# Attention and feed-forward in one kernel: w_out loaded in two column parts, the weight fold moved behind the scores of batch 0, batches 1 and 2 moved among the outputs of group 0

## The chip, the cores and the metric

The kernel runs on one core of a Trainium2 chip. The metric is the device time of one execution in microseconds (us). A core has five engines with their own instruction queues, each worked off in order: TensorE (PE: matmuls, with weight loads beside them, PEld), VectorE (DVE), ScalarE (ACT), GpSimd (POOL) and SyncE (SP). DMA transfers are issued from the queues of POOL, SP and ACT; those that change the type on the way (all loads here, float32 to float16) are issued from POOL. Engines wait for one another by semaphores. Matmul results go to PSUM, eight banks of 512 float32 per partition.

## The reference

Sliding-window causal attention over 8 batches, 8 heads, 576 positions and head size 64 gives the rows of x; a feed-forward part follows. Cut to what matters:

```python
scores = (q @ k.T) / sqrt(64)
mask = (rel >= 0) & (rel < 64)              # rel = query position - key position
attn = softmax(where(mask, scores, -1e9))
x = (attn @ v) -> [4608 tokens, 512]        # heads side by side
a = x @ w1                                  # [512, 1024]
b = x @ w2                                  # [512, 1024]
h = a * b @ w3                              # [1024, 1024]
out = h @ w_out                             # [1024, 512]
```

## The kernel before

**The fold.** w3 and w_out are multiplied once into wc (1024 x 512), so that each token needs x @ w1, x @ w2, the product of both, and one product with wc. w3 comes in four parts of 256 rows (`load_w3`, L447), w_out in one load (`load_wo`, L441). `fold_t(fc)` transposes 128 rows of w3 in 8 matmuls against the identity (L454) and DVE copies them out (L456); `fold_mm(fc)` multiplies them with w_out in 8 matmuls (L462) and DVE or ACT copies the result into `wc_sb` (L463). There are 8 values of fc.

**Attention.** Each batch has three segments of 192 queries; segment n of all is number n (0 to 23). `load_qk` loads q or k of a batch in four transfers (L206), each row of which holds RUN = 9 positions; DVE transposes it in two halves (`transposes`, L217). `scores(n)` makes 32 small matmuls (L276) into two PSUM tiles named a_ps, of which there are only two, of two banks each. `weigh` takes the exponential of each on ACT (L286), the first for index d = 2n and the second for 2n+1. The mask is applied by two or four selections on POOL (`select`, L250 and L252); for the odd d of batches 0 and 1 (SHORT = 2) DVE multiplies with a band of ones instead (L291), made once on POOL by `make_bands`. `values(d)` multiplies with v and, in the same matmuls, with ones beside v, whose result is the sum of the weights. It uses an a_ps tile again; ACT takes the logarithm of the sum and the exponential of its negative, and DVE multiplies into xT. In batches below SHORT this has a short form with 16 matmuls, two ACT steps and one DVE step (L320 to L328); in the others 8 matmuls, three ACT steps and two DVE steps (L336 to L346). `load_v` loads v in blocks (L230), `copy_v` copies half blocks on DVE (L234, L236). `ones_of` writes the ones beside v. `keep_sums` stores the logarithms for a range check at the end.

**Feed-forward.** Nine groups g of 512 tokens. `ffn_ab(g, fc)` has 8 matmuls of 512 columns (L398) into two of the four f_ps tiles; ACT copies one out (L403) and DVE multiplies the other into `ab` (L404). For group 1 it is done in pieces of two fc and 256 tokens, first for the first token half and later for the second. `ffn_o(g, t)` makes 128 rows of the output in 8 matmuls (L416), copied out by DVE (L418) and stored from SP (L425).

**The order.** Nothing schedules by itself: each engine runs its part of the code in the order in which the code is written. `keep_busy` runs matmuls on the identity at the start. Then come the loads, the scores of batch 0 between the steps of the fold, values of batch 0, `ffn_ab(0)`, and the outputs of group 0 with batch 1 among them. From there on the order is a loop over slots (one ffn_ab or ffn_o each, with a due time), after each of which ticks u run while they are due. There are 12 ticks to a batch: tick 4n calls `scores(n)` with both exponentials, the two ticks after it `values` of the segment before, and the table `late` says in which tick of a batch the loads, transposes and copies of the next batches are issued. All loads of the program share eight semaphores in turn, so a load is issued only when the eighth load before it has landed, and what stands behind it in POOL's queue waits with it.

Of the kernel before, what the change touches and what calls it, by code (L numbers as in the profile page):

```python
# [9 lines left out]
FP16 = mybir.dt.float16  # L10
# [5 lines left out]
P = 128  # L16
# [128 lines left out]
def kernel(  # L145
# [52 lines left out]

    RUN = 9

    def load_qk(b, which):
        src = k if which == "k" else q
        r = RUN
        t = sb.tile([P, 2, TI * D], FP16, name=which + "16", bufs=2)
        for j in range(NJ):
            nc.gpsimd.dma_start(  # L206
                out=t[32 * j:32 * j + 32].rearrange("p hh (i n) -> p (hh i) n", n=r * D),
                in_=src[b, 2 * j:2 * j + 2].rearrange("hh (i p r) d -> p (hh i) (r d)", p=32, r=r))
        t16s[which, b] = t
# [51 lines left out]

    def scores(n):
# [20 lines left out]
    def weigh(d, s_ps, si, w):  # L283

# [63 lines left out]
    def keep_sums(n):  # L348
# [4 lines left out]

    late = {1: [("t", 1, "k", 0)], 3: [("t", 1, "q", 0), ("v", 1, 0, 2, 3)],
            5: [("t", 1, "k", 1), ("v", 1, 4, 5)], 6: [("load", 2, "k")], 7: [("t", 1, "q", 1)],
            8: [("copy", 1, 4)], 9: [("copy", 1, 1)], 10: [("load", 2, "q")]}

# [8 lines left out]
    def tick(u):  # L366
# [82 lines left out]
    def fold_t(fc):  # L449
# [40 lines left out]
    nc.scalar.preload_act_table_set("natural_log_exp_and_others")  # L490
    make_identity(nc, ident16)
# [6 lines left out]
    def fold_step(fc):  # L498
        if fc + 1 < 8:
            w3Ts[fc + 1] = fold_t(fc + 1)  # L500
        fold_mm(fc, w3Ts.pop(fc), act_cp if fc % 4 == 3 else dve_cp)
# [8 lines left out]
    ones_of(0, nc.vector)  # L510
    make_bands()
    ones_of(1, nc.gpsimd)
    keep_busy(100)
    for hh in range(2):
        transposes(0, "k", hh)
        transposes(0, "q", hh)
# [3 lines left out]
    load_w3(3)  # L520
    w3Ts[0] = fold_t(0)
    fold_step(0)
    scores(1)
# [10 lines left out]
    copy_v(0, 1)
    fold_step(4)
    copy_v(0, 4)
    values(0)
    values(1)
    fold_step(5)
    values(2)  # L540
    values(3)
    fold_step(6)
    values(4)
    values(5)
    fold_step(7)
# [11 lines left out]
    transposes(1, "q", 0)
    transposes(1, "q", 1)
    scores(3)
    load_qk(2, "q")  # L560
# [6 lines left out]
    load_v(2, 0, 2, 3, 4, 5)
    ffn_o(0, 2)
    store()
    scores(5)  # L570
    values(8)
    values(9)
# [4 lines left out]
    for fc in range(0, 8, 2):
        ffn_ab(1, fc, 2, 0, 256)
        transposes(2, "kq"[fc // 4], fc // 2 % 2)
        if fc in (2, 4):  # L580
            values(9 + fc // 2)
# [71 lines left out]
```

## Time and profile before

| | us |
|---|---|
| median of 3 runs | 295.2 |
| lowest, highest | 294.61, 295.31 |
| the profiled execution | 294.81 |
| its span in the trace | 293.1 |
| PE busy | 262.6 |
| DVE, POOL, ACT busy | 182.8, 175.8, 149.6 |

The profile is of one execution. Its times are microseconds from the start of the span. A line such as L398 is a line of the kernel before. The mean granted clock of TensorE is 0.961 of full speed; the two levels are 1.2 and 2.4 GHz, so that a mean between 0.5 and 1 is a mix of both.

### The profile page before, as it was taken

How to read it: one execution, taken by the hardware profiler on the slowest of the kernel's cores; microseconds unless marked ns; L12 is line 12 of the kernel's file. 1: busy time of each engine (PE TensorE's matmuls, PEld its weight loads, DVE VectorE, ACT ScalarE, POOL GpSimd, SP SyncE). 2: the span in 40 equal slices, each digit the busy share in tenths (PEclk: the TensorE clock that was granted, in tenths of full speed). 3: DMA queues.
4: the chain of work that ended last, by engine and by line, in shares of the span. 5: the costliest groups of instructions: out<-in, count | busy, mean ns of one | idle time of the engine just before them, and what ended most of it. 6: DMA issues, size and time to landing. Idle time of an engine off the chain costs nothing.

```text
span 293.1 us, 6430 instructions
## 1 busy us (share of the span) xinstructions
PE 262.6 (90%) x2518; PEld 151.2 (52%) x2518; DVE 182.8 (62%) x272; ACT 149.6 (51%) x256; POOL 175.8 (60%) x243
## 2 busy tenths in 40 slices
PE   7729999962899579999999999999999999999992
PEld 7624564421478445545554498554545554454442
DVE  3424674556479557778688847766988655645531
ACT  1023264322745825786677576567658875551310
POOL 8894927209762997878779872957765554104000
PEclk9968999996899959999999999999999999999998
DMA  6999999916983778859885668395843012003013
GB/s 80 182 211 155 183 192 173 114 38 118 117 141 64 46 66 148 151 35 146 173 74 48 121 170 55 28 226 85 54 85 90 4 38 108 1 2 144 1 39 113
DMA packets 56419, 29.45 MB, mean 100 GB/s; under 512 B 39312, under 2 KB 50832, under 8 KB 56384
## 3 DMA queue, kind: packets, MB, share of 16 engines
q0 software_dynamic: 50960, 19.41, 60.7%
q1 hardware_dynamic: 5280, 9.46, 8.9%
q8 instruction: 21, 0.34, 0.5%
q14 instruction: 14, 0.11, 0.1%
q10 hardware_dynamic: 144, 0.13, 0.1%
HBM read 38.80 MB, written 9.44 MB: 165 GB/s over the span
## 4 chain that ended last, share of the span: by engine, by line
PE 79%; DVE 6%; DMA 4%; ACT 4%; issue 2%; POOL 2%; DVEq 0%; POOLq 0%
PE f_ps L398 40%; PE f_ps L416 21%; PE a_ps L276 5%; PE f_ps L462 5%; PE a_ps L336 4%; DMA ab<-in_moe_w_dram 4%; ACT pt L286 2%; PE a_ps L320 2%; DVE kT L217 1%; PE f_ps L454 1%; DVE xT L346 1%; POOL k L206 1%; DVE qT L217 1%; POOL q L206 1%; DVE ab L404 1%
## 5 line engine op out<-in xcount | busy, mean ns | idle before, releaser
L398 PE MATMUL f_ps<-xT,w_sb 128*128 128x512 f16 (+1 forms) x704 | 132.3, 340 | 0.8 <-DVE ab L404 0.8
L398 PEld LDWEIGHTS <-w_sb 128*128 128x128 f16 x704 | 66.6, 98 | 52.3 <-issue 2.7
L250 POOL TENSOR_SCALAR_AFFINE_SELECT pt<-pt 128x1024 f16<-128x1024 f16 (+2 forms) x56 | 45.9, 819 | 61.6 <-ACT pt L286 61.6
L286 ACT ACTIVATE pt<-a_ps 128x1024 f16<-128x1024 f32 (+1 forms) x48 | 43.1, 950 | 64.4 <-PE a_ps L276 64.4
L404 DVE TENSOR_TENSOR ab<-f_ps,a_sb 128x512 f16<-128x512 f32 x72 | 49.4, 690 | 36.2 <-PE f_ps L398 20.4
L416 PE MATMUL f_ps<-wc_sb,ab 128*128 128x512 f16 (+1 forms) x296 | 69.3, 384 | 0.1
L403 ACT COPY a_sb<-f_ps 128x512 f32<-128x512 f32 x72 | 41.9, 582 | 36.6 <-PE f_ps L398 36.6
L252 POOL TENSOR_SCALAR_AFFINE_SELECT pt<-pt 128x1024 f16<-128x1024 f16 (+2 forms) x56 | 46.6, 833 | 3.8
L416 PEld LDWEIGHTS <-ab 128*128 128x128 f16 x296 | 28.2, 100 | 31.8 <-issue 3.0
L230 POOL DMA_DIRECT2D v<-in_v_dram x40 | 34.0, 859 | 0.6 <-PE f_ps L416 0.2
L345 DVE TENSOR_TENSOR xT<-a_ps,r 64x384 f16<-64x384 f32 x36 | 19.7, 546 | 23.5 <-ACT r L344 23.5
L418 DVE COPY t2k<-f_ps 128x512 f32<-128x512 f32 (+1 forms) x36 | 24.2, 681 | 12.7 <-PE f_ps L416 12.1
L276 PE MATMUL a_ps<-qT,kT 32*128 32x128 f16 (+1 forms) x768 | 17.2, 214 | 9.7 <-DVE qT L217 5.6
L342 ACT ACTIVATE ln_s<-a_ps 64x384 f32<-64x384 f32 x36 | 17.6, 488 | 13.2 <-PE a_ps L336 12.2
L336 PEld LDWEIGHTS <-v 128*128 128x128 f16 x288 | 18.5, 99 | 8.6 <-issue 2.0
L217 DVE STREAM_TRANSPOSE kT<-k 128x576 int32<-128x576 int32 x16 | 19.5, 1221 | 5.4 <-DMA k<-in_k_dram 5.1
L276 PEld LDWEIGHTS <-kT 32*128 32x128 f16 x768 | 12.6, 94 | 19.5 <-issue 17.6
L336 PE MATMUL a_ps<-pt,v 128*128 128x128 f16 (+1 forms) x288 | 21.1, 217 | 1.3 <-POOL pt L252 1.3
L206 POOL DMA_DIRECT2D q<-in_q_dram x32 | 17.7, 559 | 7.0 <-DMA w_sb<-in_moe_w_dram 6.9
L346 DVE TENSOR_TENSOR xT<-a_ps,r 64x384 f16<-64x384 f32 x36 | 20.2, 560 | 0.5
L217 DVE STREAM_TRANSPOSE qT<-q 128x576 int32<-128x576 int32 x16 | 19.2, 1208 | 1.8 <-DMA q<-in_q_dram 1.7
L206 POOL DMA_DIRECT2D k<-in_k_dram x32 | 17.8, 564 | 2.8 <-issue 1.7
(46 smaller groups left out, 171.4 us busy)
## 6 DMA issues: line engine op xcount, KB each, us to landing
out_dram<-t2k SPq DMA_DIRECT2D x35, 256.0 KB
k<-in_k_dram POOLq DMA_DIRECT2D x32, 144.0 KB, 4.9
q<-in_q_dram POOLq DMA_DIRECT2D x32, 144.0 KB, 4.6
v<-in_v_dram POOLq DMA_DIRECT2D x32, 128.0 KB, 4.6
w_sb<-in_moe_w_dram POOLq DMA_DIRECT2D x4, 512.0 KB, 7.8
ab<-in_moe_w_out_dram POOLq DMA_DIRECT2D x1, 1024.0 KB, 11.5
ab<-in_moe_w_dram POOLq DMA_DIRECT2D x2, 512.0 KB, 13.8
xT<-in_moe_w_dram POOLq DMA_DIRECT2D x2, 512.0 KB, 13.2
```

Of the source, the lines that this page charges most:

```text
L206: nc.gpsimd.dma_start(out=t[32 * j:32 * j + 32].rearrange("p hh (i n) -> p (hh i) n", n=r * D), in_=src[b, 2 * j:2 * j + 2].rearrange("hh ...
L217: nc.vector.transpose(dst[b][:, hh].rearrange("q t c -> q (t c)").bitcast(I32).rearrange("q (i p r) -> q i r p", p=32, r=r), t16s[which, b ...
L230: nc.gpsimd.dma_start(out=vh[lo:P, c], in_=v[b, :, s0:s0 + P - lo, :].rearrange("h s d -> s h d"))
L250: nc.gpsimd.affine_select(out=sl, in_=sl, pattern=pat, compare_op=ALU.is_ge, fill=0.0, base=off, channel_multiplier=-1)
L252: nc.gpsimd.affine_select(out=sl, in_=sl, pattern=[[-s, m] for s, m in pat], compare_op=ALU.is_ge, fill=0.0, base=63 - off, channel_multip ...
L276: nc.tensor.matmul(s_ps[j // 2][:, j % 2, o0:o0 + m], kT[part, a, k0:k0 + P, c], qT[part, a, q0:q0 + m, c], start=(c == 0), stop=(c == 1), ...
L286: nc.scalar.activation(pt[:, :, :, 0:w], s_ps, AF.Exp, bias=-SHIFT, scale=scale)
L336: nc.tensor.matmul(o_ps[:, jj, o0:o0 + n], v16[:, si * 2 + bi, j0 + jj, a * D:a * D + P], pt[:, jj, a, c0:c0 + n], start=first, stop=(bi = ...
L398: nc.tensor.matmul(d[:, f * n + c0:f * n + c1], w[:, dc, (fc + f) * P:(fc + f + 1) * P], xT[:, dc, xc:xc + c1 - c0], start=first, stop=(dc ...
L403: act_cp(a_sb[:, 0:nf * n], a_ps[:, 0:nf * n])
L404: nc.vector.tensor_tensor(ab[:, fc:fc + nf, lo:hi], b_ps[:, 0:nf * n].rearrange("p (f n) -> p f n", f=nf), a_sb[:, 0:nf * n].rearrange("p ...
L416: nc.tensor.matmul(o_ps[:, 0:c1 - c0], ab[:, fc, t * P:t * P + P], wc_sb[:, fc, c0:c1], start=(fc == 0), stop=(fc == 7))
```

## The change

w_out is loaded in two halves of its columns, and the first four products of the fold are done by halves. The bands are made between the loads of w3's first and second part, the identity after the loads of k, and the ones of both v tiles on DVE. scores(1) and scores(2) come between the transposes and the products of the fold; the results of the fold are copied by ACT alone. All transposes of batch 1 lie inside ffn_ab(0); scores(3), (4) and (5) stand between the outputs of group 0 and its values behind them, together with the transposes of batch 2; k and q of batch 2 are loaded before that in one row. The first scores of batch 2 move between the first pieces of group 1. Batch 2 takes the short form of values (SHORT = 3), but the band product on DVE stays with batches 0 and 1 (EARLY = 2). In the loop the second exponential of a segment is issued a tick later (tick 4n+1), and the table `late` puts the transposes into ticks 3, 4, 7 and 8. Batches 3 to 7 load q and k with rows of RUN = 2 positions. The third output of group 0 is copied by ACT.

```diff
-    SHORT = 2
+    SHORT = 3
+    EARLY = 2
-    RUN = 9
+    RUN = [9] * 3 + [2] * (B - 3)
...
+        r = RUN[b]
...
         for jp in range(2):
-            weigh(2 * n + jp, s_ps[jp].rearrange("k j (a n) -> k j a n", a=2)[:, :, :, 0:w], si, w)
+            held[2 * n + jp] = s_ps[jp].rearrange("k j (a n) -> k j a n", a=2)[:, :, :, 0:w]
+        weigh(2 * n)
+        if now:
+            weigh(2 * n + 1)
...
-        if d % 2 == 1 and d < 6 * SHORT:
+        if d % 2 == 1 and d < 6 * EARLY:
...
-    late = {1: [("t", 1, "k", 0)], 3: [("t", 1, "q", 0), ("v", 1, 0, 2, 3)],
+    late = {3: [("t", 1, "k", 0), ("v", 1, 0, 2, 3)], 4: [("t", 1, "q", 0)],
...
         if m == 0 and n < NS:
-            scores(n)
+            scores(n, now=False)
+        if m == 1 and n < NS:
+            weigh(2 * n + 1)
...
-    def ffn_o(g, t):
+    def ffn_o(g, t, cp=dve_cp):
...
-    def load_wo():
-        nc.gpsimd.dma_start(out=wo16, in_=moe_w_out.rearrange("(e p) m -> p e m", p=P))
+    def load_wo(half):
+        cols = slice(half * 256, half * 256 + 256)
+        nc.gpsimd.dma_start(out=wo16[:, :, cols], in_=moe_w_out[:, cols].rearrange("(e p) m -> p e m", p=P))
...
-    def fold_mm(fc, w3T, cp):
+    def fold_mm(fc, c0, c1, cp):
         o_ps = ps_f.tile([P, DM], FP32, name="f_ps")
         for ec in range(8):
-            nc.tensor.matmul(o_ps, w3T[:, ec, :], wo16[:, ec, :], start=(ec == 0), stop=(ec == 7))
-        cp(wc_sb[:, fc, :], o_ps)
+            nc.tensor.matmul(o_ps[:, c0:c1], w3Ts[fc][:, ec, :], wo16[:, ec, c0:c1], start=(ec == 0), stop=(ec == 7))
+        cp(wc_sb[:, fc, c0:c1], o_ps[:, c0:c1])
...
+    keep_busy(120)
     scores(0)
+    keep_busy(30)
+    fold_t(0)
+    fold_t(1)
+    scores(1)
...
+    fold_mm(0, 0, 256, act_cp)
+    fold_mm(1, 0, 256, act_cp)
+    fold_t(2)
+    fold_t(3)
+    scores(2)
...
-            ahead = (LAG + 1) * (min(1, (i + 1) / 4) if g == 1 else 1)
-            slots.append((w, lo + (hi - lo) * (i + 1) / len(part) + ahead))
-    u = 24
+            due = lo + (hi - lo) * (i + 1) / len(part) + LAG + 1
+            slots.append((w, [28, 29, 30, 32, 33, 34, 36, 37][i] if g == 1 else due))
+    u = U0
```

Where the order changes, the rows of the engines' queues show it. First POOL at the start of the program, from the load of w_out on (tile ab is w_out or w3, as the right side says; band is the mask of ones). Before:

```order
L441 DMA ab_83<-in_moe_w_out_dram 128x8x512
L447 DMA ab_84<-in_moe_w3_dram 128x2x1024 x2
L447 DMA xT_77<-in_moe_w3_dram 128x2x1024
L230 DMA v16_0_79<-in_v_dram 128x8x64 x3
L259 MEMSET band_0_81 128x256
```

And now:

```order
L461 DMA ab_83<-in_moe_w_out_dram 128x8x256
L467 DMA ab_84<-in_moe_w3_dram 128x2x1024
L267 MEMSET band_0_81 128x256
L258 AFFINE_SELECT band_0_81<-band_0_81 128x128
L260 AFFINE_SELECT band_0_81<-band_0_81 128x128
L258 AFFINE_SELECT band_0_81<-band_0_81 128x64
L260 AFFINE_SELECT band_0_81<-band_0_81 128x64
L267 MEMSET band_1_82 128x256
L258 AFFINE_SELECT band_1_82<-band_1_82 128x256
L260 AFFINE_SELECT band_1_82<-band_1_82 128x256
L467 DMA ab_84<-in_moe_w3_dram 128x2x1024
L461 DMA ab_83<-in_moe_w_out_dram 128x8x256
```

Half of w_out moved behind the second part of w3, and the bands from behind the loads to between them.

Next DVE around the outputs of group 0 (t2k is an output on its way out, kT and qT the transposed k and q, pt the weights, ab the product of the feed-forward). Before, from the last pieces of ffn_ab(0) on:

```order
L217 STREAM_TRANSPOSE kT_801<-k16_494 128x2x9x32
L404 TENSOR_TENSOR ab_722<-f_ps_818,a_sb_827 128x512
L418 COPY t2k_830<-f_ps_831 128x512
L217 STREAM_TRANSPOSE qT_842<-q16_499 128x2x9x32 x2
L291 TENSOR_TENSOR pt_885<-pt_885,band_0_81 128x4x192
L418 COPY t2k_893<-f_ps_894 128x512
L291 TENSOR_TENSOR pt_943<-pt_943,band_1_82 128x1024
L234 COPY v16_1_80<-v16_1_80 64x8x64
L236 COPY v16_1_80<-v16_1_80 64x8x64
L328 TENSOR_TENSOR xT_77<-a_ps_948,r_950 128x2x192
```

And now, from the copies of v on:

```order
L242 COPY v16_1_80<-v16_1_80 64x8x64
L308 TENSOR_TENSOR pt_932<-pt_932,band_0_81 128x4x192
L437 COPY t2k_935<-f_ps_936 128x512
L308 TENSOR_TENSOR pt_985<-pt_985,band_1_82 128x1024
L437 COPY t2k_991<-f_ps_992 128x512
L308 TENSOR_TENSOR pt_1041<-pt_1041,band_1_82 128x1024
L225 STREAM_TRANSPOSE kT_1044<-k16_879 128x2x9x32
L345 TENSOR_TENSOR xT_77<-a_ps_1058,r_1060 128x2x192
L225 STREAM_TRANSPOSE kT_1044<-k16_879 128x2x9x32
L345 TENSOR_TENSOR xT_77<-a_ps_1081,r_1082 128x2x192
L437 COPY t2k_1104<-f_ps_1105 128x512
```

The transposes of batch 1 (q16_499 before) left this place, the copies of v moved ahead of the bands, and the transposes of batch 2 (k16_879) stand between the products into xT.

Last ACT at the same place (a_ps is the input of an exponential into pt, or of the logarithm of values). Before:

```order
L286 ACTIVATE pt_939<-a_ps_905 128x1024
L286 ACTIVATE pt_943<-a_ps_906 128x1024
L326 ACTIVATE ln_s_949<-a_ps_948 128x384
L327 ACTIVATE r_950<-ln_s_949 128x384
L326 ACTIVATE ln_s_949<-a_ps_970 128x384
L327 ACTIVATE r_971<-ln_s_949 128x384
L286 ACTIVATE pt_1042<-a_ps_1008 128x1024
L286 ACTIVATE pt_1046<-a_ps_1009 128x1024
```

And now:

```order
L303 ACTIVATE pt_981<-a_ps_947 128x1024
L303 ACTIVATE pt_985<-a_ps_948 128x1024
L303 ACTIVATE pt_1037<-a_ps_1003 128x1024
L303 ACTIVATE pt_1041<-a_ps_1004 128x1024
L437 COPY t2k_1046<-f_ps_1047 128x512
L343 ACTIVATE ln_s_1059<-a_ps_1058 128x384
L344 ACTIVATE r_1060<-ln_s_1059 128x384
L343 ACTIVATE ln_s_1059<-a_ps_1081 128x384
```

All exponentials of batch 1 moved ahead of the first logarithm of its values.

## Rows read from the trace of the kernel before

**Rows 1.** Busy time by stages: stretch, its length, engines busy, PEclk granted, DMA share, GB/s

```profile
12.20:20.30 8.10, 0.75 (x33) 0.56 (x32) 3.81 (x4) 1.51 (x2) 7.61 (x14) 0.83 1.19 209
20.30:45.10 24.80, 24.26 (x288) 14.01 (x289) 14.32 (x25) 10.21 (x17) 14.12 (x19) 0.92 1.53 180
24.00:28.00 4.00, 4.00 (x61) 1.98 (x62) 0.95 (x2) 1.94 (x2) 1.13 (x2) 0.96 3.08 139
45.10:61.00 15.90, 15.82 (x73) 7.04 (x72) 8.15 (x12) 5.27 (x9) 6.96 (x10) 1.00 1.26 119
61.00:92.30 31.30, 21.71 (x328) 15.10 (x327) 20.66 (x28) 13.94 (x23) 17.82 (x25) 0.89 0.82 111
92.30:115.40 23.10, 18.02 (x189) 11.50 (x178) 14.63 (x23) 12.90 (x21) 21.40 (x29) 0.85 0.64 68
115.40:288.00 172.60, 171.39 (x1483) 92.44 (x1482) 117.05 (x182) 104.49 (x183) 97.56 (x128) 1.00 0.50 84
```

**Rows 2.** What PE waited for: us in total, times, longest us

```profile
PE a_ps L276 <- DVE qT L217: 5.6, 4, 1.9
...
PE a_ps L320 <- DVE v L236: 4.3, 1, 4.3
PE a_ps L276 <- DVE xT L346: 4.0, 3, 2.8
```

**Rows 3.** Chain of waits up to ffn_ab(0): start us, us, what

```profile
7.14 13.12 DMA ab<-in_moe_w_dram
...
20.30 1.89 PE f_ps L454 x16
22.19 2.90 PE f_ps L462 x8
...
25.67 0.55 PE f_ps L454 x8
26.22 1.73 PE f_ps L462 x8
...
39.12 1.01 PE a_ps L320 x32
...
43.43 1.83 PE f_ps L462 x8
45.26 13.93 PE f_ps L398 x64
```

**Rows 4.** DMA issues of the page: count, KB each, median us to landing

```profile
ab<-in_moe_w_out_dram POOLq DMA_DIRECT2D x1, 1024.0 KB, 11.5
```

**Rows 5.** Timeline and chain: start us, us, engine, operation, idle before and releaser

```profile
9.34 1.22 DVE L217 STREAM_TRANSPOSE kT<-k 128x576 int32<-128x576 int32 x1 [5.11 <-DMA k<-in_k_dram]
...
42.56 0.55 POOL L206 DMA_DIRECT2D q<-in_q_dram  x1 [3.80 <-DMA w_sb<-in_moe_w_dram]
...
66.76 1.95 ACT pt L286 x2
```

**Rows 6.** Chain of waits among the outputs of groups 0 and 1

```profile
66.09 0.62 PE a_ps L276 x32
...
81.65 3.49 PE f_ps L398 x32
...
87.57 0.57 PE a_ps L320 x16
...
105.48 3.53 PE f_ps L416 x8
...
111.56 0.45 PE a_ps L336 x8
```

**Rows 7.** Busy time in one batch of the steady part, columns as in rows 1

```profile
115.39:141.93 26.54, 26.11 (x242) 13.26 (x243) 20.67 (x33) 18.38 (x32) 21.38 (x30) 1.00 0.79 110
```

**Rows 8.** Issues of q and v on POOL: duration ns min/median/max, first and last start

```profile
L206 POOL DMA_DIRECT2D q<-in_q_dram x32: 545/545/642, 4.1 to 200.1; - x32
L230 POOL DMA_DIRECT2D v<-in_v_dram x40: 704/892/910, 10.2 to 216.5; - x40
```

More of the change, by code (lines that the diff above doesn't have):

```diff
@@ L197, with load_qk @@
     t16s, kTs, qTs = {}, {}, {}
-    RUN = 9
-    def load_qk(b, which):
+    RUN = [9] * 3 + [2] * (B - 3)
+    def load_qk(b, which, *hhs):
         src = k if which == "k" else q
[L203 to L209, printed above, removed]
+        r = RUN[b]
+        if (which, b) not in t16s:
+            t16s[which, b] = sb.tile([P, 2, TI * D], FP16, name=which + "16", bufs=2)
+        t = t16s[which, b]
+        if not hhs:
+            for j in range(NJ):
+                nc.gpsimd.dma_start(
+                    out=t[32 * j:32 * j + 32].rearrange("p hh (i n) -> p (hh i) n", n=r * D),
+                    in_=src[b, 2 * j:2 * j + 2].rearrange("hh (i p r) d -> p (hh i) (r d)", p=32, r=r))
+        for hh in hhs:
+            for i in range(2):
+                nc.gpsimd.dma_start(
+                    out=t[:, hh, i * r * D:(i + 1) * r * D],
+                    in_=src[b, hh:H:2, i * 32 * r:(i + 1) * 32 * r].rearrange("j (p r) d -> j p (r d)", p=32, r=r))
     def transposes(b, which, hh):
         dst = kTs if which == "k" else qTs
-        r = RUN
+        r = RUN[b]
         if hh == 0:
@@ L260, in make_bands, with scores @@
             select(bands[i].unsqueeze(1), i)
-    def scores(n):
+    held = {}
+    def scores(n, now=True):
         b, si = divmod(n, 3)
@@ L351, in keep_sums @@
         nc.sync.dma_start(out=lnsum[2 * n:2 * n + 2, :], in_=y[0:P:D].rearrange("a j n -> a (j n)"))
[L354 to L356 removed]
+    late = {3: [("t", 1, "k", 0), ("v", 1, 0, 2, 3)], 4: [("t", 1, "q", 0)],
+            5: [("v", 1, 4, 5)], 7: [("t", 1, "k", 1), ("load", 2, "k")], 8: [("t", 1, "q", 1), ("copy", 1, 4)],
+            9: [("load", 2, "q")], 11: [("copy", 1, 1)]}
     def event(b, kind, ahead, *a):
@@ L410, in ffn_o @@
         r0 = g * GT + t * P
-        halves = [(0, DM, dve_cp)] if (g, t) != (NG - 1, 3) else [(0, 256, act_cp), (256, DM, dve_cp)]
+        halves = [(0, DM, cp)] if (g, t) != (NG - 1, 3) else [(0, 256, act_cp), (256, DM, dve_cp)]
         for c0, c1, cp in halves:
@@ L490 @@
     nc.scalar.preload_act_table_set("natural_log_exp_and_others")
-    make_identity(nc, ident16)
     def ones_of(i, engine):
@@ L496 @@
     w3Ts = {}
[L498 to L501, printed above, removed]
     load_qk(0, "k")
+    make_identity(nc, ident16)
     load_qk(0, "q")
-    load_wo()
+    load_wo(0)
     load_w3(0)
+    make_bands()
     load_w3(1)
+    load_wo(1)
     load_w3(2)
     load_v(0, 0, 2, 3)
[L510 to L516, printed above, removed]
@@ L517 @@
-    keep_busy(40)
-    scores(0)
-    load_v(0, 4, 5)
[L520 to L523, printed above, removed]
+    for i in range(2):
+        ones_of(i, nc.vector)
+    for which in "kq":
+        for hh in range(2):
+            transposes(0, which, hh)
+    keep_busy(120)
+    scores(0)
+    keep_busy(30)
+    fold_t(0)
+    fold_t(1)
+    scores(1)
+    load_w3(3)
+    load_v(0, 4, 5)
+    fold_mm(0, 0, 256, act_cp)
+    fold_mm(1, 0, 256, act_cp)
+    fold_t(2)
+    fold_t(3)
@@ L524 @@
+    scores(2)
     for i in range(2):
         load_w12(i, 0)
-    fold_step(1)
-    scores(2)
+    fold_mm(2, 0, 256, act_cp)
+    fold_mm(3, 0, 256, act_cp)
+    fold_mm(0, 256, DM, act_cp)
+    fold_mm(1, 256, DM, act_cp)
+    fold_t(4)
+    fold_t(5)
+    fold_mm(2, 256, DM, act_cp)
+    fold_mm(3, 256, DM, act_cp)
+    copy_v(0, 1)
+    fold_mm(4, 0, DM, act_cp)
+    values(0)
+    values(1)
+    fold_t(6)
+    fold_mm(5, 0, DM, act_cp)
+    values(2)
+    values(3)
+    copy_v(0, 4)
+    fold_t(7)
@@ L528 @@
+    fold_mm(6, 0, DM, act_cp)
+    values(4)
+    values(5)
+    fold_mm(7, 0, DM, act_cp)
     for i in range(2):
         load_w12(i, 1)
-    fold_step(2)
-    fold_step(3)
     load_qk(1, "k")
     load_qk(1, "q")
[L534 to L545, printed above, removed]
     load_v(1, 0, 2, 3, 4, 5)
-    load_qk(2, "k")
     for n in range(3):
         keep_sums(n)
-    for fc in range(6):
+    for fc in range(8):
@@ L551 @@
         ffn_ab(0, fc)
-    for fc in range(6, 8):
-        transposes(1, "k", fc - 6)
-        ffn_ab(0, fc)
+        if 2 <= fc < 6:
+            transposes(1, "kkqq"[fc - 2], fc % 2)
+    load_qk(2, "k")
+    load_qk(2, "q")
+    copy_v(1, 1)
+    copy_v(1, 4)
+    scores(3)
     ffn_o(0, 0)
     store()
[L557 to L560, printed above, removed]
+    scores(4)
+    load_v(2, 0, 2, 3)
     ffn_o(0, 1)
     store()
-    scores(4)
-    copy_v(1, 1)
+    scores(5)
@@ L565 @@
+    transposes(2, "k", 0)
+    ffn_o(0, 2, act_cp)
+    store()
     values(6)
+    transposes(2, "k", 1)
     values(7)
[L567 to L572, printed above, removed]
+    load_v(2, 4, 5)
     ffn_o(0, 3)
     store()
-    copy_v(1, 4)
+    values(8)
+    transposes(2, "q", 0)
+    values(9)
     load_qk(3, "k")
[L577 to L581, printed above, removed]
+    load_qk(3, "q")
@@ L582 @@
+    ffn_ab(1, 0, 2, 0, 256)
+    values(10)
+    transposes(2, "q", 1)
+    ffn_ab(1, 2, 2, 0, 256)
+    values(11)
+    for n in range(3, 6):
+        keep_sums(n)
+    U0 = 24
+    ffn_ab(1, 4, 2, 0, 256)
+    tick(24)
+    tick(25)
     copy_v(2, 1)
     copy_v(2, 4)
-    load_qk(3, "q")
-    for n in range(3, 6):
-        keep_sums(n)
+    ffn_ab(1, 6, 2, 0, 256)
+    tick(26)
+    U0 = 27
     need = [12 * B if g == NG - 1 else 12 * g + 4 * -(-(GT - 64 * g) // 192) for g in range(NG)]
```

10 lines of the change are left out of this document (6 added, 4 removed).

## The prediction

> **What bounds the kernel now.** I read the span cut into stages first, then what TensorE (PE) waited for, then the chain of waits. From 115.4 us on, PE is busy 171.4 of 172.6 us at a granted clock of 1.00 [rows 1]: whatever the other engines do there, at most 1.2 us can be had. Before that there are three weak stretches: 12.2 to 20.3 (PE busy 0.75 of 8.1 us), 61.0 to 92.3 (21.7 of 31.3, clock 0.89) and 92.3 to 115.4 (18.0 of 23.1, clock 0.85). Between the first two PE is busy nearly all the time [rows 1]. So the kernel is bound by PE's own work, plus some 25 us of the first 115 in which PE waits or runs slowly, and there the change has to be priced. Behind the waits stand other engines: transposes of q on VectorE (DVE), copies of v on DVE, and the DVE products that free the a_ps buffers (5.6, 4.3 and 4.0 us) [rows 2].
>
> The profiled execution took 294.8 us (span 293.1 and 1.7 around it), the median of the runs is 295.2. What I work out in the trace is taken off the median.
>
> **Part 1, the start and the fold.** In the chain, the load of w3's first part is issued at 7.14 and lands 13.12 later, at 20.3; then the first transposes of the fold start [rows 3]. All of w_out (1024 KB) stands ahead of it in the queue [rows 4]; in the new order only one column half does. In 12.2 to 20.3 the queue moved 209 GB/s [rows 1], so 512 KB are 2.5 us and the transposes can start at 17.8. The other bound: shorter rows may move more slowly, and the slowest stretch, the one with the v loads, moved 139 GB/s [rows 1]; then the half takes 3.8 us and the start is at 19.1. I take 209, since a half row of w_out is still four times a row of v. The bands now stand between w3's first and second part on GpSimd; the queue holds data until 17.8, so that costs nothing.
>
> From there to the first matmul of ffn_ab(0) the old order took from 20.3 to 45.3 [rows 3]. The work in it at full clock: 8 transpose groups at 0.55 (4.4), 8 products at 1.73 to 1.83, on average 1.78 (14.2), 2 scores at 0.62 (1.2), 3 pairs of values at 1.01 (3.0): 22.8 us [rows 3, 6]. The rest of the 25.0 is mostly the clock: 16 transposes took 1.89 and the first product 2.90, where 1.10 and 1.73 would do [rows 3], that is 2.0. The new order has four products in two halves, four more pieces at 0.1 each (1.83 against 1.73 after a change of kind): 23.2. It puts scores(1) and scores(2) between transposes and products, which gives loads and copies time, and it copies out on ScalarE (ACT), where nothing is late. So ffn_ab(0) starts at 17.8 + 23.2 = 41.0 instead of 45.3: **-4.3 us**. The identity behind the k loads and the second memset on DVE cost nothing: DVE waits 5.11 us for k there [rows 5] and the memset is as long as the one already in front of it. Without that wait the memset would delay the transposes by its own length.
>
> **Part 2, group 0's outputs, up to the first piece of group 1's second token half.** ffn_ab(0) takes 13.9 us [rows 3] and ends at 54.9 instead of 59.2. All four transposes of batch 1 now lie inside it; what they need is q of batch 1. In the old kernel its third load was issued only at 42.56, after a wait of 3.80 for the weights [rows 5]. By the bytes between w3's first part and it (5.4 MB at 209 GB/s and 0.6 MB of v at 139) it is in at 48, with pauses as in the old queue at 51; DVE reaches it at 51. That is tight, but PE has two products ahead there. Then, up to the point at which the old kernel stood at 92.3, PE has: scores 4 x 0.62 = 2.5; outputs 4 x 1.83 = 7.3; values 6 x 0.57 = 3.4; half pieces of ffn_ab(1) 5 x 1.85 (3.49 for two, and 0.1) = 9.2 [rows 3, 6]: 22.4 us. The waits that I find in walking it: scores(5) waits for the second exponential of scores(4) (a pair takes 1.95 [rows 5], the output between them 1.83): 0.3. values(9) needs the a_ps buffer of values(7), and DVE does a transpose of 1.22 [rows 5] between their two products: 0.65 to 1.2. scores(6) waits 0.1 for values(11). Together 1.6. GpSimd's selection for values(6) stands behind q of batch 2 in its queue, from some 56 on; PE asks for it at 62. So 24.0 us in place of 92.3 - 59.2 = 33.1: **-9.1 us**. Batch 2's selections stay on GpSimd, which has room (part 4).
>
> **Part 3, the rest of group 1.** From 92.3 to 115.4 the old kernel waits behind two exponentials, the ACT steps of values, transposes and xT, and afterwards runs at the lower clock (3.53 for 8 output matmuls that take 1.83 at full clock [rows 6]). The same work: 3 half pieces at 1.85, 2 scores at 0.62, 4 values at 0.57, 4 outputs at 1.83: 16.4 us of 23.1. In the new order every a_ps buffer is free before the scores that want it: **-6.7 us**. Batch 2 in the short form costs PE 0.57 instead of 0.45 for each values [rows 6], inside this sum.
>
> **Part 4, the steady part.** The second exponential is now queued one tick later, transposes in ticks without values. ACT has the same work (18.4 of 26.5 us per batch [rows 7]), the a_sb copy goes ahead, and values(2n-1) asks for the buffer some 2 us after that exponential. Gain between 0 and 1.2, loss up to 0.3 for the last two short values: **-0.3 us**. Batches 3 to 7 are loaded in runs of two rows, 576 pieces for each load instead of 128. An issue with 128 pieces takes 0.55 us, the v load with 1024 takes 0.89 and its half 0.70 [rows 8], so 576 are 0.73; 8 issues a batch add 1.4 to GpSimd's 21.4 of 26.5 us [rows 7]: hidden, at 22.8.
>
> **The sum.** -4.3 - 9.1 - 6.7 - 0.3 = -20.4, that is 274.8. I add 0.7 for small hand-overs that the walk does not see: **275.5 us**. Bounds of this case: 272.5 (no waits in part 2, all 1.2 in part 4) to 278 (the start at 19.1, and 1 us more of waits).
>
> **Rival A, the clock falls at the start.** Between the warm-up matmuls and the first transposes PE again does little, from about 12 to 17.8. In the old kernel it did 0.75 us of work in 8.1, the granted clock was 0.83 on average [rows 1], and the slow start of the fold cost 2.0 (part 1). Against it: 30 more warm-up matmuls stand behind scores(0). If it falls all the same, and the half of w_out is slow too, the time is 275.5 + 2.0 + 1.3, about 279. The Trainium skill (TensorE: Matmul & The Clock Gate, section "HAM oscillation — how this bites in real kernels") says that idle gaps throttle the array and that each return to full speed is paid again; by it the time would be this rival's. The trace agrees so far, in that each of its dips follows an idle stretch.
>
> **Rival B, the output stretch still waits.** k, q, v of batch 1 and k, q of batch 2 stand in one row on GpSimd ahead of the first selection of batch 1, and GpSimd waits for earlier loads (3.80 us once [rows 5]). If q of batch 1 lands 3 us later than 51, scores(3) waits, PE idles, and the clock falls as in 61 to 92. Half of parts 2 and 3 (15.8) would stay: 283.4. Against it: the queue has the same bytes ahead as before, and fewer pauses.
>
> **Rival C, slower.** If an issue costs by the piece, 576 pieces take 4.5 x 0.55 = 2.5 us, and GpSimd needs 21.4 + 8 x 1.95 = 37 us a batch. Then selections are late and PE waits 10.5 us in each of five batches: 275.5 + 52, about 328. It delays PE from 0.55 + 5.1/8 = 1.19 us per issue on, and the kernel is slower than before from about 1.7. The v rows speak against it [rows 8].
>
> **How the numbers follow.** Forecast 0.60. Rival A 0.15 (279), rival B 0.15 (283.4), rival C 0.05; 0.02 for no change in time, because the stages before 115 us only shift their waits; 0.03 for faster than 272.5. Predicted is the forecast, 275.5. The range takes in A and B and the bounds of the forecast: 272 to 284. A measurement can tell about 0.3% from no change: faster by more 0.93, within 0.02, slower 0.05.
>
> **What would show it.** First transposes of the fold near 18 us at full clock; ffn_ab(0) at 41; scores(9), at 115.4 before, at 95; no PE wait over 1.5 us between 41 and 95, and a granted clock of 1.00 there; q and k issues near 0.73 in batches 3 to 7; a steady part of 172 us. I am wrong if PE idles more than 5 us in 41 to 95, or if GpSimd's issue of q takes over 1.2 us.

## The result, and the profile after

The changed kernel takes **268.7 us** (median of 4 runs, 268.44 to 269.21), against 295.15 for the kernel before beside it (294.61 to 295.31): a ratio of 0.911, 95% interval 0.909 to 0.913. Forecast were 275.5 us and a range of 272 to 284. The direction was right, but the kernel gained 26.4 us where 19.7 were predicted, and the time lies 3.3 us below the low end. The profiled execution took 268.6 us, with a span of 266.8 against 293.1.

First the page of the kernel after: busy time, share of the span and instructions of each engine, then from the strips over the span the one of PE and the one of the granted clock.

```profile
PE 254.4 (95%) x2608; PEld 149.7 (56%) x2608; DVE 169.7 (64%) x260; ACT 151.4 (57%) x261; POOL 178.7 (67%) x243
...
PE   3979999998999999999999999999999999999992
...
PEclk9999999999999999999999999999999999999998
```

The weak stretches of [rows 1] are gone, and the granted clock stays at its upper level, 2.4 GHz, after the start. Five stages to hold against those of [rows 1] (the stage from 54.00 begins where ffn_ab(0) ends; columns: length, then PE, PEld, DVE, ACT, POOL busy, granted clock, DMA share, GB/s):

```profile
12.00:17.40 5.40, 4.01 (x91) 3.54 (x88) 2.80 (x3) 1.51 (x2) 5.33 (x7) 1.00 1.23 209
17.40:40.10 22.70, 22.30 (x321) 16.39 (x322) 10.32 (x19) 13.84 (x27) 14.72 (x21) 1.00 1.45 194
54.00:77.00 23.00, 22.04 (x339) 15.07 (x339) 17.60 (x27) 15.87 (x26) 19.55 (x27) 1.00 1.26 158
77.00:93.00 16.00, 16.00 (x213) 9.89 (x214) 10.23 (x17) 9.39 (x15) 15.21 (x20) 1.00 0.82 77
93.00:261.60 168.60, 168.60 (x1498) 91.33 (x1498) 111.50 (x179) 104.26 (x181) 104.81 (x133) 1.00 0.63 88
```

What PE waited for, the answer to [rows 2] (us in total, times, longest):

```profile
PE f_ps L506 <- POOL ident masks.py:199: 4.6, 1, 4.6
PE a_ps L337 <- DVE xT L345: 0.8, 1, 0.8
PE f_ps L474 <- DMA ab<-in_moe_w_dram: 0.7, 1, 0.7
PE a_ps L286 <- DVE qT L225: 0.7, 1, 0.7
PE a_ps L337 <- DVE v L242: 0.3, 1, 0.3
```

The first row is the wait for the identity at the very start. Of the three waits of [rows 2], 5.6, 4.3 and 4.0 us, there remain 0.7, 0.3 and none. The chain of waits, answering to [rows 3] (start us, us, what):

```profile
7.51 9.87 DMA ab<-in_moe_w_dram
...
38.27 1.83 PE f_ps L481 x8
40.10 13.93 PE f_ps L417 x64
...
73.40 5.34 PE f_ps L417 x48
```

From these, where the 26.3 us of the span went. The first piece of group 1's second token half, at which the kernel before stood at 92.3, ends at 73.40 + 2/3 of 5.34 = 76.96; scores(9) starts at 92.93 in place of 115.39. The stretches, in us:

| stretch | before | after | change | predicted |
|---|---|---|---|---|
| start to ffn_ab(0) | 45.3 | 40.1 | -5.2 | -4.3 |
| to that piece of group 1 | 47.0 | 36.9 | -10.2 | -9.1 |
| to scores(9) | 23.1 | 16.0 | -7.1 | -6.7 |
| scores(9) to the end | 177.7 | 173.9 | -3.8 | -0.3 |
| allowance for hand-overs | | | 0 | +0.7 |

The largest error is in the last stage, the one which the prediction held to be full. Nearly the whole difference within it arises between scores(9) and scores(23): 128.32 us before, 124.57 after (-3.75).

### The profile page after: what moved, and what is told of

Same layout as the page of the kernel before. It is cut to its first block, busy times and chain, and to the rows that moved or that the text cites. A ratio compares the mean times of both kernels' runs of the same rounds, so it can differ in the third digit from the quotient of the medians.

```text
span 266.8 us, 6600 instructions
## 1 busy us (share of the span) xinstructions
PE 254.4 (95%) x2608; PEld 149.7 (56%) x2608; DVE 169.7 (64%) x260; ACT 151.4 (57%) x261; POOL 178.7 (67%) x243
## 4 chain that ended last, share of the span: by engine, by line
PE 87%; DMA 4%; POOL 2%; DVE 2%; ACT 2%; issue 1%; POOLq 0%; DVEq 0%
PE f_ps L417 48%; PE f_ps L435 22%; PE a_ps L353 5%; PE a_ps L286 4%; PE f_ps L481 4%; DMA ab<-in_moe_w_dram 4%; PE a_ps L337 3%; ACT pt L303 1%; PE f_ps L474 1%; POOL q L210 1%; POOL k L210 1%; DVE xT L345 1%; DVE kT L225 1%; POOL ab L461 0%; DVE pt L308 0%
## 5 line engine op out<-in xcount | busy, mean ns | idle before, releaser
L435 PE MATMUL f_ps<-wc_sb,ab 128*128 128x512 f16 (+1 forms) x296 | 66.4, 374 | 0.0
L422 ACT COPY a_sb<-f_ps 128x512 f32<-128x512 f32 x72 | 41.8, 581 | 36.9 <-PE f_ps L417 36.4
L362 DVE TENSOR_TENSOR xT<-a_ps,r 64x384 f16<-64x384 f32 x30 | 16.5, 550 | 22.0 <-ACT r L361 22.0
L210 POOL DMA_DIRECT2D q<-in_q_dram x32 | 19.7, 621 | 11.8 <-DMA w_sb<-in_moe_w_dram 8.3
L210 POOL DMA_DIRECT2D k<-in_k_dram x32 | 20.1, 634 | 1.6 <-POOLq L671 1.0
L353 PEld LDWEIGHTS <-v 128*128 128x128 f16 x240 | 15.1, 98 | 6.4
L345 DVE TENSOR_TENSOR xT<-a_ps,r 128x384 f16<-128x384 f32 x18 | 10.0, 553 | 13.0 <-ACT r L344 13.0
L359 ACT ACTIVATE ln_s<-a_ps 64x384 f32<-64x384 f32 x30 | 14.6, 487 | 5.8 <-PE a_ps L353 5.0
L353 PE MATMUL a_ps<-pt,v 128*128 128x128 f16 x240 | 17.2, 215 | 0.0
L363 DVE TENSOR_TENSOR xT<-a_ps,r 64x384 f16<-64x384 f32 x30 | 16.8, 561 | 0.4
L361 ACT ACTIVATE r<-ln_s 128x384 f32<-128x384 f32 x30 | 15.7, 523 | 1.0
L225 DVE STREAM_TRANSPOSE qT<-q 128x576 int32<-128x576 int32 x16 | 14.7, 928 | 1.6 <-DMA q<-in_q_dram 1.6
```

Source lines behind the costliest of these rows:

```text
L210: nc.gpsimd.dma_start(out=t[32 * j:32 * j + 32].rearrange("p hh (i n) -> p (hh i) n", n=r * D), in_=src[b, 2 * j:2 * j + 2].rearrange("hh ...
L353: nc.tensor.matmul(o_ps[:, jj, o0:o0 + n], v16[:, si * 2 + bi, j0 + jj, a * D:a * D + P], pt[:, jj, a, c0:c0 + n], start=first, stop=(bi = ...
L422: act_cp(a_sb[:, 0:nf * n], a_ps[:, 0:nf * n])
L435: nc.tensor.matmul(o_ps[:, 0:c1 - c0], ab[:, fc, t * P:t * P + P], wc_sb[:, fc, c0:c1], start=(fc == 0), stop=(fc == 7))
```

## Experiments

All runs had their own runs of the kernel before beside them. Where a kernel is built on the one after, its median compares with 268.7, and its stretch from scores(9) to scores(23) with 124.57.

### The steady part: which of the three edits in the loop brought 3.75 us?

The change edits the loop of the steady part in three places: the table `late` (which moves transposes, and the copies of v of its tick 9, out of the ticks that hold values), the length of a run in the loads of k and q (`RUN`), and the second exponential. First each was undone alone.

**a_late**, the table as before:

```
-    late = {3: [("t", 1, "k", 0), ("v", 1, 0, 2, 3)], 4: [("t", 1, "q", 0)],
-            5: [("v", 1, 4, 5)], 7: [("t", 1, "k", 1), ("load", 2, "k")], 8: [("t", 1, "q", 1), ("copy", 1, 4)],
-            9: [("load", 2, "q")], 11: [("copy", 1, 1)]}
+    late = {1: [("t", 1, "k", 0)], 3: [("t", 1, "q", 0), ("v", 1, 0, 2, 3)],
+            5: [("t", 1, "k", 1), ("v", 1, 4, 5)], 6: [("load", 2, "k")], 7: [("t", 1, "q", 1)],
+            8: [("copy", 1, 4)], 9: [("copy", 1, 1)], 10: [("load", 2, "q")]}
```

> The changed kernel with the old table of ticks: transposes of the next batch back in the ticks 1, 3, 5, 7 of a batch (two of them with values), loads and copies of v as before. The stretch from scores(9) to the last result is 172.5 us before and 168.8 after. Theory 1 (the place of the transposes makes the difference): this stretch goes back to 172 or more, the time to 272. Theory 2 (the transposes of batches 3 to 7 became shorter, 0.77 instead of 1.22 us, because of the shorter runs): the short transposes fit in the old place too, the stretch stays within 169.5, the time within 269.5. Theory 3 (the second exponential): no change, 268.7.

**a_run**, runs of nine rows for every batch:

```
-    RUN = [9] * 3 + [2] * (B - 3)
+    RUN = [9] * B
```

> The changed kernel with RUN = 9 for all batches, so that the transposes of batches 3 to 7 take 1.22 us again and their loads have 128 pieces. Theory 1 (place): the stretch from scores(9) stays below 169.5, the time below 269.5. Theory 2 (duration): the stretch goes to 171 to 172.5, the time to 271 to 272.5. Theory 3 (second exponential): 268.7. All: POOL issues fall from 0.65 to 0.55 us and free about 1 us a batch on POOL, worth nothing.

**a_exp**, both exponentials of a scores in one tick:

```
-            scores(n, now=False)
-        if m == 1 and n < NS:
-            weigh(2 * n + 1)
+            scores(n)
```

> The changed kernel with both exponentials of a segment in the tick of its scores again. Theory 3 (the second exponential in front of a_sb delays the product that frees an f_ps tile): the stretch from scores(9) grows from 168.8 to 171 or more, the time to 271. Theories 1 and 2: less than 0.5 us, 268.7 to 269.2.

**a_all3** undoes all three.

> The changed kernel with all three edits of the loop undone: old table of ticks, RUN = 9, both exponentials together. Start and outputs of group 0 as changed. All theories: the stretch from scores(9) is 172.2 to 172.8 us again, and the time 272.0 to 273.0; the rest of the gain (some 22 us) stays. If the stretch stays under 171, something outside these three edits makes the steady part shorter.

Two more kernels then undid two at a time: **a_laterun** has the old table and the long runs, **a_latexp** the old table and the exponentials together.

> The changed kernel with two edits of the loop undone: the old table of ticks and RUN = 9 (long transposes of 1.22 us in the old places); the second exponential stays a tick later. From scores(9) to scores(23) it is 124.6 us in the changed kernel, 127.0 with the old table alone, 128.7 with all three edits undone. If the length of a transpose matters only in a tick with values, this run has 128.3 to 128.7 and a time of 272.4 to 272.9. If the second exponential is what was missing there, it stays at 127.0 and 271.2.

> The changed kernel with the old table of ticks and both exponentials together, but short transposes (RUN = 2 for batches 3 to 7). If the length of a transpose is what mattered in the old places, scores(9) to scores(23) stay at 127.0 us and the time at 271.2. If the second exponential mattered there, 128.3 to 128.7 us and 272.4 to 272.9.

Measured:

| kernel | undone | median us | ratio to before, 95% | scores(9) to (23) |
|---|---|---|---|---|
| after | nothing | 268.7 | 0.909 to 0.913 | 124.57 |
| a_exp | exponential | 268.4 | 0.908 to 0.914 | 124.58 |
| a_run | runs | 268.4 | 0.908 to 0.915 | 124.57 |
| a_late | table | 271.3 | 0.915 to 0.923 | 127.03 |
| a_latexp | table, exponential | 271.0 | 0.913 to 0.917 | 127.03 |
| a_laterun | table, runs | 272.5 | 0.920 to 0.924 | 128.63 |
| a_all3 | all three | 272.8 | 0.922 to 0.928 | 128.68 |

The gain is the table's. The second exponential is worth nothing, with either table. Shorter runs are worth nothing beside the new table and 1.6 us beside the old one. What they shorten is the transposes on DVE (line, instruction, count, busy us and mean ns of one), first in the kernel after, then in a_run; the 928 is a mean over 1.2 us in the batches with runs of nine and 0.77 in the others:

```profile
L225 DVE STREAM_TRANSPOSE qT<-q 128x576 int32<-128x576 int32 x16 | 14.7, 928 | 1.6 <-DMA q<-in_q_dram 1.6
```

```profile
L225 DVE STREAM_TRANSPOSE qT<-q 128x576 int32<-128x576 int32 x16 | 19.1, 1202 | 1.1 <-DMA q<-in_q_dram 1.1
```

The old table costs 2.46 us with short transposes and 4.06 with long ones. That is nearly the ratio of the lengths, 0.77 to 1.22, but the agreement is chance: the two losses are not made of the same waits. Where they arise can be read by setting the 85 groups of matmuls between scores(9) and scores(23) of two runs side by side, each from its start to the start of the next, and then looking at what stands on DVE ahead of the product that PE waits for:

| run, and what it is held against | longer by, us | behind transposes | behind copies of v |
|---|---|---|---|
| a_laterun, after | 4.1 | 3.4 | 0.7 |
| a_late, after | 2.5 | 0.6 | 1.8 |
| before, b_steady (below) | 4.2 | 3.6 | 0.6 |

The copies of v are the other thing that the table moves: from tick 9, which holds values, to tick 11, which holds none. The largest single loss of a_late, 0.99 us at scores(12), is behind them, as its chain of waits shows:

```profile
116.86 0.73 DVE v L242
...
117.62 1.14 DVE v L244
...
119.95 0.57 DVE xT L363
...
120.65 0.52 PE a_ps L286 x27
```

In a_laterun the same two copies took 0.82 us in place of 1.9, and nothing was lost there; why their length differs, no run shows. Nor does a run move the copies alone, so this split is read from the traces and not tried out. A long transpose in the old place cost between nothing and about 0.8 of its 1.22 us.

What mattered for the prediction is how the trace shows these waits. The stretch from scores(9) to scores(23), one row for each of before, after and a_late (columns as above):

```profile
115.39:243.71 128.32, 127.19 (x1217) 70.69 (x1218) 94.85 (x146) 87.17 (x152) 89.58 (x121) 1.00 0.63 95
```

```profile
92.93:217.50 124.57, 124.57 (x1233) 69.67 (x1233) 89.41 (x144) 86.92 (x150) 96.84 (x126) 1.00 0.81 101
```

```profile
93.61:220.64 127.03, 126.23 (x1233) 70.42 (x1233) 89.23 (x143) 86.89 (x150) 96.81 (x126) 1.00 0.80 99
```

After and a_late have the same 1233 matmuls at the same clock, yet PE is "busy" 1.66 us longer in a_late. Of the 2.46 us only 0.8 is shown as idle. One place in the timeline of before shows how (start us, us, engine, line, what):

```profile
120.38 3.78 PE L398 MATMUL f_ps<-xT,w_sb 128*128 128x512 f16 x16
...
121.14 1.23 DVE L217 STREAM_TRANSPOSE kT<-k 128x576 int32<-128x576 int32 x1
...
122.40 0.69 DVE L404 TENSOR_TENSOR ab<-f_ps,a_sb 128x512 f16<-128x512 f32 x1
...
123.56 0.56 DVE L346 TENSOR_TENSOR xT<-a_ps,r 64x384 f16<-64x384 f32 x1
...
124.10 0.80 PE L276 MATMUL a_ps<-qT,kT 32*128 32x128 f16 x32
```

The same place with the two groups of matmuls cut where they halt (windows 123.136:124.2 and 124.33:124.8 of PE):

```profile
123.14 1.02 PE L398 MATMUL f_ps<-xT,w_sb 128*128 128x512 f16 x4
124.10 0.23 PE L276 MATMUL a_ps<-qT,kT 32*128 32x128 f16 x2
...
124.27 0.63 PE L276 MATMUL a_ps<-qT,kT 32*128 32x128 f16 x30
```

And the like place in the kernel after:

```profile
123.30 3.62 PE L417 MATMUL f_ps<-xT,w_sb 128*128 128x512 f16 x16
...
125.64 0.56 DVE L363 TENSOR_TENSOR xT<-a_ps,r 64x384 f16<-64x384 f32 x1
...
126.83 0.77 DVE L225 STREAM_TRANSPOSE kT<-k 128x576 int32<-128x576 int32 x1
...
126.85 0.64 PE L286 MATMUL a_ps<-qT,kT 32*128 32x128 f16 x32
```

In before, the 16 matmuls are drawn 3.78 long and the scores 0.80, where after they take 3.62 and 0.64: twice 0.16 us, and no idle time. Both times PE waits for a product on DVE, which the transpose of 1.23 has held up. The product into ab starts as the transpose ends and is done at 122.40 + 0.69 = 123.09; the last four of the 16 matmuls, which need the f_ps buffer that it frees, start at 123.14. The product into xT is done at 123.56 + 0.56 = 124.12. By then the first two matmuls of scores have begun, into the one a_ps buffer; the other 30 start at 124.27, since the second buffer comes free only with that product. In the kernel after, both products are done before PE asks for their buffers (the one into xT at 126.20), and the transpose (0.77) comes behind them.

Nothing of this shows as idle, because a matmul is drawn longer than it holds up the next. One of 512 columns is drawn 0.38 us, but 16 of them take 3.62 in all, one each 0.22. So a halt of up to 0.16 us is covered, and a longer one looks 0.16 shorter than it is. For the small matmuls of scores, drawn 0.23, it is that much: the 0.99 of a_late shows as 0.76. The Trainium skill (Perfetto Trace Analysis, section "Identifying the Most-Contended Engine") says that matmul busy share is no good measure of how close a kernel is to its roofline, because pipelined instructions look smaller in the trace. The trace agrees with the warning, but here the other way round: busy time held 127.19 us where 124.57 were needed.

**b_steady** is the other side of it: the kernel before with only the three loop edits (the line of `late` stands for the table, the other way round than in a_late).

```
-    RUN = 9
+    RUN = [9] * 3 + [2] * (B - 3)
...
-    late = {1: [("t", 1, "k", 0)], 3: [("t", 1, "q", 0), ("v", 1, 0, 2, 3)],
+    late = {3: [("t", 1, "k", 0), ("v", 1, 0, 2, 3)], 4: [("t", 1, "q", 0)],
...
-            scores(n)
+            scores(n, now=False)
+        if m == 1 and n < NS:
+            weigh(2 * n + 1)
```

> The kernel before with the three loop edits alone (new table of ticks, RUN = 2 for batches 3 to 7, second exponential a tick later); start and outputs as before. If the steady gain does not hang on the rest: scores(9) to scores(23) 124.6 us instead of 128.3, and 295.1 - 3.7 = 291.4 us. If the tables only fit the new start, less than 1 us is gained, 294.5.

It took 288.7 us (288.63 to 289.16), ratio 0.977, 0.975 to 0.978. From scores(9) to scores(23) it needs 0.45 us less than the kernel after, where the last two values of batch 2 have the short form, which takes PE longer:

```profile
114.63:238.75 124.12, 124.12 (x1219) 69.72 (x1219) 89.10 (x147) 87.77 (x152) 94.68 (x124) 1.00 0.78 98
```

That is 4.2 us less than before, where "at most 1.2" had been read. Its span fell by 5.7 us; the other 1.5 are 0.8 up to scores(9), 0.5 of it because the fold's first transposes start earlier (19.76 for 20.30), and 0.7 after scores(23); I can't put either down to the edits. The medians differ by 7.0 us; the part beyond the profiled executions is not explained.

### The outputs of group 0 and group 1: is it the order?

**a_out** keeps the new start and the new loop but has the old order from the loads of batch 1 to the loop (a cut; the rows left out go the same way, and group 1's due times are the old ones):

```
-        if 2 <= fc < 6:
-            transposes(1, "kkqq"[fc - 2], fc % 2)
...
-    copy_v(1, 1)
-    copy_v(1, 4)
-    scores(3)
...
+    transposes(1, "q", 0)
+    transposes(1, "q", 1)
+    scores(3)
+    load_qk(2, "q")
```

> The changed kernel with the order of before from the loads of batch 1 to the loop (outputs of group 0, batches 1 and 2 among them, slots of group 1), but start, short form and loop edits as changed. From the first matmul of ffn_ab(0) to scores(9) it was 70.1 us before and is 52.9. If the order of this stretch makes the difference: 68 to 70 us again, waits of PE on transposes of q and copies of v, a granted clock under 0.9 there, and 284 to 286 us. If what helped is that the loads are earlier by the shorter start, or the short form for batch 2: 60 us or less and under 277.

It took 283.3 us (282.98 to 285.31), ratio 0.961, 0.956 to 0.965: 14.6 us more than after. From ffn_ab(0) to scores(9) it needs 67.95 us, the kernel before 70.1, the kernel after 52.8. So 15.1 of the 17.3 us gained there hang on the order (with group 1's due times); the other 2.2 came with the new start, the short form or the loop, which no run separates. The waits of before are back:

```profile
PE a_ps L337 <- DVE v L244: 3.7, 1, 3.7
PE a_ps L286 <- DVE qT L225: 3.5, 4, 1.9
PE a_ps L286 <- DVE xT L345: 1.6, 1, 1.6
...
```

and so is the lower clock. These are 31 us of its outputs, to be held against the row from 61.00 in [rows 1]:

```profile
61.00:92.00 31.00, 24.57 (x318) 17.47 (x317) 19.44 (x29) 14.63 (x25) 20.09 (x28) 0.80 0.93 103
```

**a_short2** takes one small piece out of that order: batch 2 in the long form of values (`SHORT` also sets how many batches use the short one).

```
-    SHORT = 3
+    SHORT = 2
```

> The changed kernel with the long form of values for batch 2 (SHORT = 2). The short form costs PE 0.12 us more for each of six values and saves an ACT step (0.49) and a DVE step (0.55). If that saving lies beside PE's work, this run is 0.7 us faster, 268.0; if values of batch 2 hold up PE without it, it is 1 us or more slower, 269.7 and above.

269.6 us (269.01 to 269.85), ratio 0.912, 0.908 to 0.915: at most a small loss, within the intervals. Where it would come from can be seen: scores(9) to scores(10) takes 9.58 in place of 8.82, and PE waits there (0.98 us, and 1.26 one scores earlier) for the products into xT:

```profile
PE a_ps L286 <- DVE xT L363: 2.2, 2, 1.3
```

### The start: the half of w_out, and the clock

**a_wo** loads both halves of w_out ahead of w3:

```
     load_wo(0)
+    load_wo(1)
     load_w3(0)
     make_bands()
     load_w3(1)
-    load_wo(1)
```

> The changed kernel with both halves of w_out loaded ahead of w3's first part; all else as changed. If what stands ahead of w3's first part in the queue sets the start of the fold, its first transposes start 2.5 us later, at 19.9 instead of 17.4, the clock may fall in the longer wait, ffn_ab(0) starts at 42.5 to 44.5 and the time is 271 to 273. If the fold is bound by a later load, less than 1 us is lost.

272.7 us (272.31 to 273.52), ratio 0.923, 0.919 to 0.926: 4.0 us more than after. Its timeline at the first transposes (in brackets, idle time and who ended it), then its granted clock around them:

```profile
20.51 1.89 PE L474 MATMUL f_ps<-ident,ab 128*128 128x128 f16 x16 [4.08 <-DMA ab<-in_moe_w_dram]
```

```profile
16.00:20.00 4.00, 0.43 (x8) 0.26 (x5) 0.71 (x1) 0.20 (x1) 2.23 (x4) 0.86 1.16 211
20.00:24.00 4.00, 3.49 (x52) 2.91 (x53) 1.38 (x2) 0.59 (x1) 0.00 (x0) 0.50 1.22 205
```

The load lands 3.1 us later than in after (17.43). PE, nearly idle for the four us ahead, then works four us at 0.50 of the full clock, that is at 1.2 GHz. ffn_ab(0) starts at 45.38, where the kernel before had 45.26. This is the longest of its four executions (273.52). In it, with all of w_out in front, the rest of the new start (halved products, scores between transposes and products, copies on ACT) gains nothing: part 1 is the half of w_out and the clock that comes with it.

**a_nokb** leaves out only the second warm-up, the 30 matmuls behind scores(0); their product is not used by anything.

```
-    keep_busy(30)
```

> The changed kernel without the 30 matmuls on the identity behind scores(0). If they keep the clock up (rival A of the prediction), the granted clock falls in the idle stretch before the fold, its first 16 transposes take 1.8 to 1.9 us instead of 1.07, ffn_ab(0) starts at 42 instead of 40.1 and the time is 270.5. If the clock holds without them, the fold starts at the same time, since it waits for w3: 268.7.

269.85 us in the median, but from 267.96 to 270.76; ratio 0.915, 0.911 to 0.919, which overlaps that of after. The profiled execution was the one of 267.96, with the first transposes at full clock:

```profile
17.16 1.07 PE L474 MATMUL f_ps<-ident,ab 128*128 128x128 f16 x16 [2.73 <-DMA ab<-in_moe_w_dram]
```

Its mean clock was 0.997; those of the other four were 0.990 to 0.994, with 1.1 to 2.8 us more time. A fall of the clock at the start fits, but of these four only the mean clock is known. The fall does occur even with the 30 matmuls: a_latexp, which changes nothing at the start, shows it in its profiled execution.

```profile
17.99 1.79 PE L472 MATMUL f_ps<-ident,ab 128*128 128x128 f16 x16 [1.98 <-DMA ab<-in_moe_w_dram]
```

There 16 transposes take 1.79, and ffn_ab(0) starts at 42.01, 1.9 us later than in after. So these matmuls do not rule the fall out; that they make it rarer is likely from the mean clocks, and not shown: with them and the same start, 2 of 33 executions of eight kernels lie below 0.995; without them, 4 of 5.

**v_best** follows from this: w3's first part ahead of any of w_out, so that there is hardly a gap, and no second warm-up (also short runs from batch 2 on).

```
-    load_wo(0)
     load_w3(0)
+    load_wo(0)
...
-    keep_busy(30)
```

> A version that tries for more: w3's first part loaded ahead of w_out's first half, no matmuls on the identity behind scores(0) (the transposes of the fold take that place), and runs of two positions for batch 2 as well. If the start is set by the first data that the fold can use, its transposes start at 15 instead of 17.4, ffn_ab(0) 1 to 1.7 us earlier, and the short transposes of batch 2 take away PE's wait of 0.8 among the outputs: 266.2 to 267. If the second operands (w_out's half, then w3's second part) set the pace of the fold, only the 0.8 is gained: 268.

**266.7 us** (266.57 to 267.76), ratio 0.904, 0.900 to 0.908: below the interval of after, about 2 us faster than it. The transposes follow scores(0) without a gap:

```profile
13.90 0.69 PE L286 MATMUL a_ps<-qT,kT 32*128 32x128 f16 x32
14.53 1.07 PE L474 MATMUL f_ps<-ident,ab 128*128 128x128 f16 x16
```

Of the 2.9 us by which they are earlier, 1.35 reach ffn_ab(0) (38.75). At scores(9) (90.96) it is 2.0, which holds what the short runs of batch 2 bring, not separated. A wait for the copies of the transposed w3 takes some of what is lost on the way:

```profile
PE f_ps L481 <- DVE w3T L476: 0.8, 1, 0.8
```

## Why the prediction was right or wrong

**Part 4 failed.** It read the 171.4 us of PE busy in [rows 1] as PE's own work and wrote that "at most 1.2 us can be had". The experiments show 4.2 us to be had there by the loop edits alone (b_steady), and of these the table brings nearly all (a_late, a_laterun). What it took for work were waits of PE for products on DVE that stand behind transposes and copies of v. Held against b_steady, 1.8 us of the 4.2 lie inside scores, which wait for the a_ps buffer that a product into xT frees, and 2.4 in the groups of ffn_ab and ffn_o, which wait for the product into ab. Only 1.1 of the 128.32 us was shown as idle. Of the three edits the part argued chiefly from the exponential, which is worth nothing; the move of the transposes it named without a price, that of the copies not at all. What would have spoken up is the chain of waits of before, read in [rows 6] up to 111.56. Between scores(9) and scores(23) it goes through a transpose three times. Here is one of them, and then the idle time that PE shows there, by what ended it:

```profile
130.12 0.92 DVE kT L217
...
131.39 0.70 DVE ab L404
...
132.13 1.02 PE f_ps L398 x4
```

```profile
PE f_ps L398 <- DVE ab L404: 0.8, 2, 0.4
PE a_ps L276 <- DVE xT L346: 0.2, 1, 0.2
```

The step cost 3.5 of the 6.6 us of error in the span. The last two short values cost 0.45 us there, where "up to 0.3" had been allowed.

**Part 1 was right in mechanism and 0.9 us short.** The queue moved 209 GB/s as taken, the load landed at 7.51 + 9.87 = 17.4 instead of 17.8, the clock held in the profiled execution, and the fold took 22.7 instead of 23.2. a_wo bears out both terms: 3.1 us of load, and 2.2 of clock (24.9 us of fold in place of 22.7), where 2.5 and 2.0 had been written.

**Part 2 was right and 1.1 us short.** Predicted were 22.4 us of work and 1.6 of waits from the end of ffn_ab(0); the row of 54 to 77 shows 22.04 busy and 1.0 idle. Of the named waits the one of values for its buffer was there (0.8 us, forecast 0.65 to 1.2). The open point, whether q of batch 1 is there in time, went well: scores(3) starts at 53.96 behind ffn_ab(0), without idle time.

**Part 3 was right.** 16.4 predicted, 16.0 measured, PE busy in all of it, clock 1.00.

**The 0.7 us for hand-overs** were not there. Parts 2 and 3 had been made from rows that already hold some; that this is why, is an argument and not shown.

**The rivals.** A, the fall of the clock, was not in the profile of after but is real: it stood once in a profiled execution with the same start (1.9 us later, 2.0 predicted), and in a_wo. B, that the outputs still wait, did not happen; a_out shows what the old order costs in full, 14.6 us, where the sum had 15.8 for parts 2 and 3 and B left half of that. C, an issue that costs by the piece, fell:

```profile
95.01 2.62 POOL L210 DMA_DIRECT2D q<-in_q_dram  x4
```

One issue of 576 pieces takes 0.65 us, below the 0.73 estimated from [rows 8]. POOL came closer to its limit than the 22.8 of 26.5 us written, without PE waiting for it; in the first batch of the loop it stood at:

```profile
93.00:118.55 25.55, 25.55 (x260) 12.84 (x264) 19.19 (x30) 17.61 (x30) 24.84 (x33) 1.00 1.14 133
```

The range failed with its low end: 272.5 took in all that Part 4 thought possible, so a false bound cut off the side on which the time then fell. (By its own terms that bound is 273.0 with the 0.7 for hand-overs and 272.3 without; the difference is too small to matter.)

## What to carry to other kernels

A PE that is busy in every row can still be waiting. Before "busy" is used as a bound, measure a group of matmuls from its start to the start of the next, at two places with the same work; where one is longer, look at what stands on the other engine ahead of the product that frees its buffer. The chain of waits names the larger of these places. A long instruction that nobody waits for belongs in a stretch in which its engine has no product that another engine wants; in the wrong place it can cost a good part of its length, or nothing. When a table moves several things at once, one that was moved in passing can bring the larger share, as the copies of v do beside short transposes. In a prologue, ask of every load ahead of the first needed one whether all of it must be there: the bytes cost once (3.1 us in a_wo), and the clock that falls in the gap can cost most of that again (2.2).

## What the runs showed of the hardware

A stream transpose of 128x576 int32 took 1.2 us for batches loaded in runs of nine rows and 0.77 for those in runs of two; its shape is the same, only the order of what it reads and writes differs. The change's short runs go with less work on DVE (89.4 us from scores(9) to scores(23) against 94.8 in a_run) and 4.3 us more on POOL (96.8 against 92.6), and neither shows in the time. A copy of v on DVE (64x512 float16) took from 0.28 to 1.16 us within the one execution of the kernel after; what sets this was not tried. The clock at the start is not settled by the program alone: executions of kernels with the same start ran the first 16 transposes in 1.07 us or in 1.79.
